# A re-dealt start-up of a fused sparse-attention and MLP kernel: load order, transposes, early scores and weight sums

## The chip, the core and the metric

The kernel runs on one core of a Trainium2 chip. TensorE (PE) multiplies, with its weight loads (PEld) beside it; VectorE (DVE), ScalarE (ACT) and GpSimd (POOL) do the elementwise work; POOL also issues the loads from memory, and SyncE (SP) the stores and the transposes by DMA. The metric is the device time of one execution in microseconds (us). Before the change the median of three runs was 321.06 us (319.18 to 321.56).

## The reference

Attention over 8 batches, 8 heads, 576 positions and head size 64, and then a two-layer MLP on the 4608 tokens that it gives. Heads 0 to 3 see a window of 32 positions ("local"); heads 4 to 7 see the earlier positions that are equal modulo 32 ("strided").

```python
mask_local = (rel >= 0) & (rel < stride)                      # stride = 32
mask_strided = (rel >= 0) & (pos[None, :] % stride == pos[:, None] % stride)
scores = np.where(masks, scale * q @ k.T, -1e9)
x = softmax(scores) @ v                                       # to 4608 x 512
h = x @ w_in                                                  # 512 x 2048
g = h * np.tanh(np.log1p(np.exp(h)))                          # Mish
out = g @ w_out                                               # 2048 x 512
```

## The kernel before

**Tiling.** The MLP works on 9 blocks of 512 tokens. Each block has a first product (x by `w_in`, into `gT` through Mish on ACT) and a second one (`gT` by `w_out`). From block 2 on the first product, and in all blocks the second, is done with seven half-size products instead of eight, which need sums of weights (`w_in_sums`, L343, into `wis` and into `w_in` itself; `w_out_sums`, L424, into `wos` and into `w_out` itself) and of activations (`x_sum`, L359; `g_sum`, L444, into `gs`); all these sums are two-input DVE instructions (L119). Blocks 0 and 1 use the ordinary first product, `plain` (L595): 16 column groups fc of 128, each four matmuls over the row groups cc; row groups 2 and 3 are the strided heads, 0 and 1 the local ones.

The second product of a block is 14 steps, called M1 to M14 below (`Mlp2.half`, L456): eight matmuls each, two steps for each of the seven products. In block 0 their order is n = 1, 2, 5, 6, 7, 3, 4. M1 and M2 need the first half of `w_out`, M3 (n = 2) the second half and a copy be<-al of what M2 left; M5 needs the changed `w_out` (sum w1), M7 the sums g1 and w2, M9 the sums w0 and g2, M11 the sum w3, M13 the sum g3.

**Attention**, one batch ahead of the MLP, in small steps put between the matmuls. For a batch, kind s (strided) or l (local): transposes of k and q; scores (`qk`) in three parts S0, S1, S2 and L0, L1, L2, each followed by two exps on ACT (L265) and a multiplication with the mask (`mask`, L271, on POOL or DVE); products with v (`pv`, L294) in five strided steps s0 to s4 and four local ones l0 to l3, each followed on DVE by a reciprocal (L298) and a multiplication (L303); and transposes of the result (`xt`) into `xT`: X0, X1 strided, Y0, Y1 local. `spread_v` and `share_v` (DVE copies) lay v out; s0 and its like need the first.

Batches 0 and 1 are transposed on PE (`t_step`, L189: 8 transposes for s, 12 for l, and a copy out of PSUM); for them raw k and q of batch 1 are kept in the tiles `hh` (strided), `xs` and a tile of the output pool (local), which have their own use only later. From batch 2 on `transpose_by_dma` (L174) does it from SP's queue.

**Order.** Everything runs in the order in which it is written, engine by engine (`manual_schedule`, L512). Loads go through POOL's queue in the order of L528 to L539, then L571, L576 and L614. The second product of block 0 is a written plan (L656): M is the next step, S0:CP is part S0 into PSUM pair C with the mask on POOL (D: DVE), k0:BD a transposing step into bank B copied by DVE, s0:B a pv step, X0:BA an xt step copied by ACT, v the laying out of v for batch 1 and the load of the next v, T the transposes by DMA, E the table load for exp on ACT, g2 and g3 sums of activations. Block 1 follows the plan SECOND (L737; p is a column group of `plain`, y its Mish, q0 to q5 the six score parts of batch 2 in the order S0 to S2, L0 to L2, all masked on POOL, v the next of the 13 pv and xt steps, k0 to k7 the sums of `w_in`, f the table load for Mish, n the sum g0), and from block 2 on MAIN (L732), where m is an M step of the block before, x0 to x3 the sums of x, and a to d and U, W, H the first product. Steps of v that a plan doesn't reach follow at its end.

PSUM has eight banks: SETS[0] and SETS[1] (be, al, ee each) and at0, at1 (A0, A1). B0 and B1 are the two be banks; pair A is A0 and A1, pair C the al and ee of SETS[0].

Of the kernel before, what the change touches and what calls it, by code (L numbers as in the profile page):

```python
# [12 lines left out]
AF = mybir.ActivationFunctionType  # L13
# [4 lines left out]
WQ = 96  # L18
CL, PL = 6, 96
SU = 80  # L20
# [25 lines left out]
def kernel(ctx, tc, q, k, v, moe_w_in, moe_w_out, out):  # L46
    nc = tc.nc
    B, H, S, D = q.shape
# [6 lines left out]
    PE, Po, Dv, Sc = nc.tensor, nc.gpsimd, nc.vector, nc.scalar  # L55
# [56 lines left out]
    def cast(eng, out_, in_):  # L112
        if eng is Sc:
            Sc.copy(out_, in_)  # L114
        else:
            eng.tensor_copy(out_, in_)
# [48 lines left out]
    def load_w_out(c0, c1):  # L165
        Po.dma_start(w_out[:, c0:c1, :], moe_w_out.rearrange("(fc p) o -> p fc o", p=128)[:, c0:c1, :])
# [7 lines left out]
    def transpose_by_dma():  # L174
        for src, dst in ((ks, kTs), (qs, qTs)):
            nc.sync.dma_start_transpose(
                dst[:, 0:16 * SU].rearrange("c (u n) -> c u n", u=16),
                src[0:SU].rearrange("p h x -> p (h x)"),
            )
        for src, dst, n in ((kl, kTl, 128), (ql, qTl, WQ)):  # L180
            nc.sync.dma_start_transpose(
                dst[:].rearrange("c (u n) -> c u n", u=12),
                src[0:n].rearrange("p h i d -> p (h i d)"),
            )
# [251 lines left out]
    class Mlp2:  # L436
# [19 lines left out]
        def half(self, n, u):  # L456
            z = (self.t + 1) % 2
            be, al, E = [x[:] for x in SETS[z]]
            W = lambda kk, j: w_out[:, 8 * kk:8 * kk + 8, 256 * j:256 * j + 256]
            G = self.G  # L460
            L, R, bank, start = {
                1: (G(0, 0), W(0, 0), al, True), 2: (G(0, 1), W(1, 0), be, False),
                3: (G(1, 1), wos[:, 2], E, False), 4: (gs[:, 1], W(1, 1), al, False),
                5: (gs[:, 0], W(0, 1), E, True), 6: (gs[:, 1], wos[:, 0], al, False),
                7: (gs[:, 2], wos[:, 1], al, False),
            }[n]
            for c in range(8):
                mm(
                    bank[:, 256 * u:256 * u + 256], L[:, c, 128 * u:128 * u + 128], R[:, c, :],
                    start=(start and u == 0 and c == 0), stop=(c == 7),  # L470
                )
            if u == 0:
                return
            r = 512 * self.t
            halves = lambda x: x.rearrange("p (u d) -> p u d", u=2)
            if n == 1:
                Sc.copy(be, al)
            elif n == 5:
                Sc.copy(o5[:], E)
            elif n == 6:  # L480
                Sc.copy(o2[:], al)
            elif n == 3:
                osb = self.out_tile(1)
                add(Dv, osb[:, :, 0:256], halves(E), halves(o2[:]))
            elif n == 7:
                osb = self.out_tile(1)
                add(Dv, osb[:, :, 256:512], halves(al), halves(o5[:]))
            elif n == 4:
                osb = self.out_tile(0)
                Sc.copy(osb[:, :, 0:256], halves(be))  # L490
                Sc.copy(osb[:, :, 256:512], halves(al))
                self.store(0)
# [19 lines left out]
    with tc.manual_schedule():  # L512
# [17 lines left out]
        load_vl(0)  # L530
        for c in range(4):
            load_w_in(512 * c, 512 * c + 512)
        load_w_out(0, 8)
        load_str(1, "ks", k)
        load_str(1, "qs", q)
        load_w_out(8, 16)
        load_loc(1, "kl", k, 128)
        load_loc(1, "ql", q, WQ)
        load_vl(1)  # L539

        Dv.memset(kTs[:, 0:16 * SU].rearrange("p (u n) -> p u n", u=16)[:, :, PN:], 0.0)
# [30 lines left out]
        a.bias("l", 0, PAIRS[1])  # L572
        a.bias("l", 1, PAIRS[2])
        t_step(0, "l", "q", 0, B0, Sc)
        t_step(0, "l", "q", 1, B1, Sc)
        load_qk(2)  # L576
        a.qk("l", 0, PAIRS[1], True)
        a.pv("s", *PV_S[0], A0)
# [27 lines left out]
        S2 = (2, 3)  # L606
        L2 = (0, 1)
# [18 lines left out]
        C = SETS[0]  # L626

        def go(plan):
            bank = {"A": A0, "a": A1, "B": B0, "C": C[1], "c": C[2]}
            eng = {"A": Sc, "D": Dv, "P": Po}  # L630
            for w in plan.split():
                f, x = w.split(":") if ":" in w else (w, "")
                if f == "M":
                    ms.pop(0)()
                elif f[0] in "kq" and f[1] in "01":
                    t_step(1, "l", f[0], int(f[1]), bank[x[0]], eng[x[1]])
                elif f[0] in "SL":
                    a.qk(f[0].lower(), int(f[1]), PAIRS[0] if x[0] == "A" else PAIRS[1])
                    a.mask(f[0].lower(), int(f[1]), eng[x[1]])
                elif f[0] in "sl":  # L640
                    n = int(f[1])
                    a.pv(f[0], *(PV_S if f[0] == "s" else PV_L)[n], bank[x])
                elif f[0] in "XY":
                    a.xt("s" if f[0] == "X" else "l", int(f[1]), bank[x[0]], eng[x[1]])
                elif f[0] == "g":
                    m2.g_sum(int(f[1]), Dv)
                elif f == "E":
                    Sc.preload_act_table(AF.Exp)
                elif f == "v":
                    spread_v(Dv)  # L650
                    share_v(1, Dv)
                    load_vs(2)
                elif f == "T":
                    transpose_by_dma()
# [90 lines left out]
        )  # L745

        for t in range(1, NBLK):
            run(SECOND if t == 1 else MAIN if t + 1 < B else PLAIN, t)
        last = Mlp2(NBLK - 1)
        st = last.steps((1, 5, 6, 2, 7, 3, 4))  # L750
        last.g_sum(1, Dv)
# [35 lines left out]
```

## Time and profile before

| What | us |
|---|---|
| median of three runs | 321.06 (319.18 to 321.56) |
| the profiled execution, its own time | 319.21 |
| its span, first to last instruction | 317.4 |
| PE, DVE, ACT, POOL busy | 288.6, 205.7, 201.2, 116.9 |
| local half of block 0's first product begins | 25.57 |
| second product of block 0 begins (M1) | 40.45 |
| local half of block 1's first product begins | 65.86 |
| M1 in block 2 begins | 90.56 |
| M1 in block 3 begins | 126.56 |
| M1 in block 4 begins | 156.37 |

Times in the profile count from the start of the span. The last five rows are where the timeline has the first matmul of that piece; the pieces between them are the stages that the change touches. In a line of the timeline the two numbers in front are start and duration, x is how many instructions were merged, and the bracket is how long the engine had been idle and what ended that.

### The profile page before, as it was taken

What the parts mean: (1) busy time and instruction counts of PE and PEld (TensorE: products, weight loads), DVE (VectorE), ACT (ScalarE), POOL (GpSimd) and SP (SyncE); (2) the same over time, 40 slices, a digit from 0 to 9 for tenths busy, and PEclk for the clock granted to TensorE, in tenths of its full rate; (3) what the DMA queues carried; (4) which work ended last, traced back from release to release, by engine and by line L of the source; (5) the groups of instructions that cost most, each with busy time, mean ns of one, the idle gap of its engine ahead of it and who ended that gap; (6) DMA issues with size and microseconds to landing.
All of it is one profiled execution on the core that took longest, in us unless ns stands there. A gap on an engine that the chain in (4) does not pass through costs nothing.

```text
span 317.4 us, 7701 instructions
## 1 busy us (share of the span) xinstructions
PE 288.6 (91%) x3218; PEld 228.4 (72%) x3224; DVE 205.7 (65%) x378; ACT 201.2 (63%) x357; POOL 116.9 (37%) x94
## 2 busy tenths in 40 slices
PE   8879679986994999999999999999999999999983
PEld 3554356833473798888888888988898887787773
DVE  2370396833888578768867794779578657747641
ACT  2587364357461768987887888788868526625630
POOL 8422355349504680298049607800930000000000
PEclk9999998999899899999999999999999999999999
DMA  7999999998990899589939993990030030002003
GB/s 105 182 206 206 204 183 138 95 243 130 150 115 0 114 231 169 32 142 214 169 41 176 205 137 64 213 107 0 2 134 2 0 119 15 3 34 101 0 2 133
DMA packets 97555, 35.85 MB, mean 113 GB/s; under 512 B 80800, under 2 KB 92896, under 8 KB 97520
## 3 DMA queue, kind: packets, MB, share of 16 engines
q0 software_dynamic: 60192, 17.67, 61.7%
q1 hardware_dynamic: 37184, 17.57, 27.7%
q8 instruction: 25, 0.41, 0.5%
q10 hardware_dynamic: 144, 0.12, 0.1%
q14 instruction: 10, 0.08, 0.1%
HBM read 35.51 MB, written 9.44 MB: 142 GB/s over the span
## 4 chain that ended last, share of the span: by engine, by line
PE 58%; DVE 16%; ACT 10%; DMA 10%; issue 4%; POOL 1%; DVEq 0%; ACTq 0%; POOLq 0%
PE al L125 29%; PE ee L125 14%; PE be L125 8%; DMA hh<-in_k_dram 7%; DVE hh L119 4%; DMA ql<-in_q_dram 3%; DVE gs L119 3%; ACT s L114 2%; ACT gT L414 2%; PE at L294 2%; PE at L125 2%; ACT gT L420 2%; DVE x_l L303 2%; DVE wis L119 1%; ACT be L401 1%
## 5 line engine op out<-in xcount | busy, mean ns | idle before, releaser
L125 PEld LDWEIGHTS <-w_in 128*128 128x128 bf16 x576 | 53.9, 98 | 23.6 <-issue 9.2
L271 POOL TENSOR_TENSOR Ps<-Ps,consts_sb 72x864 bf16<-72x864 bf16 (+1 forms) x20 | 36.8, 1859 | 87.1 <-ACT Ps L265 87.1
L125 PEld LDWEIGHTS <-gs 128*128 128x128 bf16 x576 | 55.8, 99 | 13.3 <-DVE gs L119 5.8
L125 PEld LDWEIGHTS <-gT 128*128 128x128 bf16 x432 | 41.0, 98 | 6.7 <-issue 0.4
L125 PE MATMUL al<-wos,gs 128*128 128x256 bf16 x288 | 36.4, 278 | 5.4 <-DVE gs L119 5.3
L125 PEld LDWEIGHTS <-wis 128*128 128x128 bf16 x348 | 33.1, 99 | 7.9 <-issue 3.3
L119 DVE TENSOR_TENSOR gs<-gT,gs 128x2048 bf16<-128x2048 bf16 x18 | 25.2, 1398 | 20.0 <-PE al L125 15.1
L271 POOL TENSOR_TENSOR Pl<-Pl,consts_sb 128x960 bf16<-128x960 bf16 (+1 forms) x20 | 33.5, 1701 | 0.8 <-ACT Pl L265 0.7
L125 PE MATMUL al<-xs,wis 128*128 128x256 bf16 x224 | 32.4, 272 | 0.8 <-ACT be L401 0.6
L125 PE MATMUL be<-xT,w_in 128*128 128x256 bf16 (+1 forms) x157 | 30.1, 311 | 2.8 <-ACT gT L693 1.3
L414 ACT ACTIVATE gT<-hh 128x1024 bf16<-128x1024 f32 x28 | 29.8, 1065 | 0.0
L125 PE MATMUL al<-xT,w_in 128*128 128x256 bf16 (+1 forms) x150 | 27.1, 299 | 1.9 <-ACT gT L420 1.7
L298 DVE RECIPROCAL rden<-at 72x7 f32<-72x7 f32 (+2 forms) x60 | 11.2, 187 | 21.6 <-PE at L294 18.1
L401 ACT COPY be<-al 128x512 f32<-128x512 f32 x28 | 16.4, 587 | 12.5 <-PE al L125 12.5
L420 ACT ACTIVATE gT<-al 128x512 bf16<-128x512 f32 x28 | 16.8, 599 | 11.0 <-PE al L125 11.0
L119 DVE TENSOR_TENSOR gs<-gT 128x2048 bf16<-128x2048 bf16 x18 | 21.9, 1217 | 0.0
L119 DVE TENSOR_TENSOR hh<-al,s 128x512 f32<-128x512 f32 x28 | 19.2, 684 | 2.9 <-PE al L125 2.5
L119 DVE TENSOR_TENSOR hh<-ee,s 128x512 f32<-128x512 f32 x28 | 19.2, 684 | 2.8 <-ACT s L114 1.9
L303 DVE TENSOR_TENSOR x_s<-at,rden 72x448 bf16<-72x448 f32 (+1 forms) x35 | 20.1, 574 | 1.2
L125 PE MATMUL ee<-wos,gT 128*128 128x256 bf16 x144 | 18.7, 277 | 0.0
L418 ACT ACTIVATE gT<-be 128x512 bf16<-128x512 f32 x28 | 15.9, 596 | 3.9 <-PE be L125 3.9
L125 PE MATMUL al<-xs,w_in 128*128 128x256 bf16 x112 | 16.8, 272 | 1.6 <-DVE hh L119 1.6
(137 smaller groups left out, 537.7 us busy)
## 6 DMA issues: line engine op xcount, KB each, us to landing
out_dram<-osb SPq DMA_DIRECT2D x18, 512.0 KB, 3.4
vraw<-in_v_dram POOLq DMA_DIRECT2D x8, 288.0 KB, 7.4
vl<-in_v_dram POOLq DMA_DIRECT2D x8, 288.0 KB, 9.6
w_in<-in_moe_w_in_dram POOLq DMA_DIRECT2D x4, 512.0 KB, 15.4
w_out<-in_moe_w_out_dram POOLq DMA_DIRECT2D x2, 1024.0 KB, 21.7
ql<-in_q_dram POOLq DMA_DIRECT2D x7, 288.0 KB, 12.9
kl<-in_k_dram POOLq DMA_DIRECT2D x5, 384.0 KB, 12.6
ks<-in_k_dram POOLq DMA_DIRECT2D x6, 288.0 KB, 10.0
```

Source lines behind the costliest of these rows:

```text
L114: Sc.copy(out_, in_)
L119: eng.tensor_tensor(out=out_, in0=a, in1=b, op=op)
L125: PE.matmul(o, lhsT=lhsT, rhs=rhs, start=start, stop=stop, skip_group_check=True)
L271: meng.tensor_tensor(out=pm, in0=pm, in1=mk[0:n, :].unsqueeze(1).unsqueeze(1).to_broadcast([n, 2, nu, w]), op=ALU.mult,)
L294: PE.matmul(po[:, n - n0, :], lhsT=pt[0:r, c0:c0 + 128], rhs=rhs, start=True, stop=True)
L298: Dv.reciprocal(rden[0:m, 0:nu], po[0:m, :, D])
L303: Dv.tensor_tensor(out=x[0:m, n0:n1, :], in0=po[0:m, :, 0:D], in1=rden[0:m, 0:nu].unsqueeze(2).to_broadcast([m, nu, D]), op=ALU.mult,)
L401: Sc.copy(be, al)
L414: Sc.activation(o[:, :, 256:512], h[:].rearrange("p i (u n) -> p (i u) n", u=2), AF.Mish)
L418: Sc.activation(o[:, 0:2, 0:256], two(be), AF.Mish)
L420: Sc.activation(o[:, 2:4, 0:256], two(al), AF.Mish)
```

## The change

It has these parts.

1. Loads: batch 1's strided k and q go ahead of the first half of `w_out`, its local k and q ahead of the second.
2. Batch 0: the copy of one local q transposition goes from ACT to DVE, where it stands behind `share_v`; the table load for Mish moves from before X0 to after the first three matmuls of block 0's first product.
3. First product of block 0: eight PSUM banks instead of six are dealt out; the strided half begins with three matmuls of row group 2 alone. Y1's copy goes to DVE. Batch 1's strided transposes follow column groups 8 to 11 (before: 9 to 12), and its local ones, which were steps k0, k1, q0, q1 of the second product's plan, follow groups 12 to 15, all copied by DVE. The sums g0 and w0 stand between the two.
4. Second product of block 0: a new plan. w1, g1, w2, w3 are spread between the steps; the copy be<-al of this block goes to DVE; the transposes by DMA come in two parts (Ts behind S2, Tl behind L2); batch 2's strided scores N0, N1, N2, masked on POOL, are added (before, q0 to q2 of block 1); the exp table is loaded at the start.
5. Block 1: q0 to q2 are gone; k1 comes early, k3 stays at the end, and k5 and k7 go to block 2, behind g3. Of the 13 v steps 12 stand in the plan; the last, Y1, follows it.

```diff
             if n == 1:
-                Sc.copy(be, al)
+                cast(Dv if self.t == 0 else Sc, be, al)
...
-        load_w_out(0, 8)
         load_str(1, "ks", k)
         load_str(1, "qs", q)
-        load_w_out(8, 16)
+        load_w_out(0, 8)
         load_loc(1, "kl", k, 128)
         load_loc(1, "ql", q, WQ)
+        load_w_out(8, 16)
         load_vl(1)
...
-        t_step(0, "l", "q", 1, B1, Sc)
+        t_step(0, "l", "q", 1, B1, Dv)
...
-        Sc.preload_act_table(AF.Mish)
...
-        for fc in range(4):
-            plain(0, fc, six[fc], S2)
-        a.xt("l", 0, A1, Sc)
-        plain(0, 4, six[4], S2)
-        plain(0, 5, six[5], S2)
-        a.xt("l", 1, A0, Sc)
+        deal = [B0, B1, A1] + SETS[1][1:] + SETS[0][1:] + [A0] + [
+            B0, B1, *SETS[1][1:], *SETS[0][1:], B0, B1
+        ]
+        for fc in range(3):
+            plain(0, fc, deal[fc], (2,))
+        Sc.preload_act_table(AF.Mish)
+        for fc in range(3):
+            plain(0, fc, deal[fc], (3,))
+        plain(0, 3, deal[3], (2, 3))
+        a.xt("l", 0, A0, Sc)
+        plain(0, 4, deal[4], (2, 3))
+        a.xt("l", 1, SETS[0][2], Dv)
+        plain(0, 5, deal[5], (2, 3))
...
         for fc in range(16):
-            plain(0, fc, six[fc % 6], (2, 3, 0, 1) if fc > 5 else L2)
-            if 9 <= fc <= 12:
-                t_step(1, "s", "kkqq"[fc - 9], fc % 2, (A0, A1)[fc % 2], Dv)
-        for n in range(4):
-            w_out_sums(n, Dv)
-            if n < 2:
-                m2.g_sum(n, Dv)
+            plain(0, fc, deal[fc], (2, 3, 0, 1) if fc > 5 else (0, 1))
+            if fc >= 8:
+                kind, n = "sl"[fc // 12], fc % 4
+                t_step(1, kind, "kq"[n // 2], n % 2, (A0, A1)[n % 2], Dv)
+            if fc == 11:
+                m2.g_sum(0, Dv)
+                w_out_sums(0, Dv)
...
         go(
-            "M M E S0:AP k0:BD S1:CP M k1:BD M S2:AD q0:BD M q1:BD M v L0:CP M g2 L1:AP s0:B M L2:CD "
-            "s1:B M M g3 s2:B M s3:A s4:a T M l0:c X0:BA M l1:C l2:A X1:aA M l3:B Y0:cA Y1:CA"
+            "E M M S0:CP w1 g1 M S1:AP M w2 M S2:CD Ts w3 v M L0:AP g2 M L1:CP s0:B M s1:B L2:AD Tl M s2:B g3 s3:A s4:a M "
+            "l0:B M X0:A l1:a M N0:CP X1:B l2:A M l3:a N1:CP Y0:B M Y1:A N2:CP"
         )
...
         SECOND = (
-            "p0 q0 p1 q1 p2 s q2 p3 q3 p4 q4 p5 v q5 f D V R y0 v v p6 v y1 p7 k0 k2 v y2 v p8 y3 k4 k6 v p9 y4 v p10 y5 v "
-            "p11 y6 v p12 y7 v p13 y8 v p14 y9 v p15 y10 y11 y12 y13 y14 y15 n k1 k3 k5 k7"
+            "p0 s p1 q3 p2 q4 p3 q5 p4 p5 f D V R v v y0 v p6 y1 v p7 v y2 p8 k0 k2 v y3 p9 k4 k6 k1 v y4 v p10 y5 v "
+            "p11 y6 v p12 y7 v p13 y8 p14 y9 v p15 y10 y11 y12 y13 y14 y15 n k3"
         )
...
+            if t == 2:
+                plan = plan.replace("g3", "g3 k5 k7")
```

More of the change, by code (lines that the diff above doesn't have):

```diff
@@ L172, in share_v, with transpose_by_dma @@
         cast(eng, vl[b % 2][0:32, :, 1:NW, 0:D], vl[b % 2][96:128, :, 0:NW - 1, 0:D])
[L174 to L184, printed above, removed]
+    def transpose_by_dma(kinds="sl"):
+        if "s" in kinds:
+            for src, dst in ((ks, kTs), (qs, qTs)):
+                nc.sync.dma_start_transpose(
+                    dst[:, 0:16 * SU].rearrange("c (u n) -> c u n", u=16),
+                    src[0:SU].rearrange("p h x -> p (h x)"),
+                )
+        if "l" in kinds:
+            for src, dst, n in ((kl, kTl, 128), (ql, qTl, WQ)):
+                nc.sync.dma_start_transpose(
+                    dst[:].rearrange("c (u n) -> c u n", u=12),
+                    src[0:n].rearrange("p h i d -> p (h i d)"),
+                )
     kTl0 = kTl[:, 0:2 * (32 + S)].rearrange("c (t n) -> c t n", t=2)
@@ L605 @@
         six = [B0, B1] + SETS[1][1:] + SETS[0][1:]
-        S2 = (2, 3)
-        L2 = (0, 1)
-        for fc in range(4):
-            plain(0, fc, six[fc], S2)
-        a.xt("l", 0, A1, Sc)
-        plain(0, 4, six[4], S2)
-        plain(0, 5, six[5], S2)
-        a.xt("l", 1, A0, Sc)
+        deal = [B0, B1, A1] + SETS[1][1:] + SETS[0][1:] + [A0] + [
[11 more added lines that the diff above has]
+        plain(0, 5, deal[5], (2, 3))
         load_vl(2)
@@ L617 @@
         for fc in range(16):
-            plain(0, fc, six[fc % 6], (2, 3, 0, 1) if fc > 5 else L2)
-            if 9 <= fc <= 12:
-                t_step(1, "s", "kkqq"[fc - 9], fc % 2, (A0, A1)[fc % 2], Dv)
-        for n in range(4):
-            w_out_sums(n, Dv)
-            if n < 2:
-                m2.g_sum(n, Dv)
+            plain(0, fc, deal[fc], (2, 3, 0, 1) if fc > 5 else (0, 1))
[5 more added lines that the diff above has]
+                w_out_sums(0, Dv)
         ms = m2.steps((1, 2, 5, 6, 7, 3, 4))
         C = SETS[0]
+        nx = Attn(2)
         def go(plan):
@@ L634, in go @@
                     ms.pop(0)()
[L635 to L639, printed above, removed]
+                elif f[0] in "SLN":
+                    at, kind = (nx, "s") if f[0] == "N" else (a, f[0].lower())
+                    at.qk(kind, int(f[1]), PAIRS[0] if x[0] == "A" else PAIRS[1])
+                    at.mask(kind, int(f[1]), eng[x[1]])
                 elif f[0] in "sl":
@@ L643, in go @@
                 elif f[0] in "XY":
-                    a.xt("s" if f[0] == "X" else "l", int(f[1]), bank[x[0]], eng[x[1]])
+                    a.xt("s" if f[0] == "X" else "l", int(f[1]), bank[x], Sc)
                 elif f[0] == "g":
                     m2.g_sum(int(f[1]), Dv)
+                elif f[0] == "w":
+                    w_out_sums(int(f[1]), Dv)
                 elif f == "E":
@@ L652, in go @@
                     load_vs(2)
-                elif f == "T":
-                    transpose_by_dma()
-        go(
-            "M M E S0:AP k0:BD S1:CP M k1:BD M S2:AD q0:BD M q1:BD M v L0:CP M g2 L1:AP s0:B M L2:CD "
-            "s1:B M M g3 s2:B M s3:A s4:a T M l0:c X0:BA M l1:C l2:A X1:aA M l3:B Y0:cA Y1:CA"
+                elif f[0] == "T":
+                    transpose_by_dma(f[1])
+        go(
+            "E M M S0:CP w1 g1 M S1:AP M w2 M S2:CD Ts w3 v M L0:AP g2 M L1:CP s0:B M s1:B L2:AD Tl M s2:B g3 s3:A s4:a M "
+            "l0:B M X0:A l1:a M N0:CP X1:B l2:A M l3:a N1:CP Y0:B M Y1:A N2:CP"
         )
@@ L747 @@
         for t in range(1, NBLK):
-            run(SECOND if t == 1 else MAIN if t + 1 < B else PLAIN, t)
+            plan = SECOND if t == 1 else MAIN if t + 1 < B else PLAIN
+            if t == 2:
+                plan = plan.replace("g3", "g3 k5 k7")
+            run(plan, t)
         last = Mlp2(NBLK - 1)
```

## The prediction

> **What bounds the kernel now.** The first page gives PE 91% busy, and the chain that ended last is 58% PE. So I asked where PE is idle, stage by stage (stretch, length, then busy time of PE, PEld, DVE, ACT, POOL, granted clock, DMA):
>
> ```profile
> 0.00:25.50 25.50, 20.83 (x255) 11.55 (x257) 10.20 (x38) 13.77 (x28) 14.21 (x21) 1.00 1.17 167
> 25.50:40.30 14.80, 12.24 (x83) 6.00 (x84) 3.62 (x6) 8.33 (x16) 4.44 (x5) 1.00 1.26 204
> 40.30:65.20 24.90, 21.67 (x303) 16.81 (x303) 19.64 (x36) 11.54 (x24) 10.41 (x7) 0.93 2.15 139
> 65.20:90.20 25.00, 20.87 (x199) 10.85 (x202) 12.26 (x28) 15.41 (x29) 15.57 (x12) 0.93 1.51 171
> 90.56:126.56 36.00, 31.19 (x365) 26.20 (x364) 27.82 (x47) 22.09 (x40) 15.95 (x12) 0.95 1.13 124
> 126.56:156.37 29.81, 29.45 (x366) 25.60 (x364) 22.48 (x43) 24.54 (x44) 16.57 (x12) 1.00 1.07 139
> ```
>
> Block 3 (last row) is PE-bound: 29.45 of 29.81 us. Block 2 does the same work in 36.0, and each earlier stage leaves PE 2.6 to 4.8 us idle. All edits lie in these stages, and what they save isn't given back, since later blocks wait on PE. The timeline names the waits that end last there:
>
> ```profile
> 12.83 0.76 POOL L133 DMA_DIRECT2D hh<-in_k_dram  x1 [1.21 <-DMA ql<-in_q_dram]
> 14.13 1.01 POOL L133 DMA_DIRECT2D hh<-in_q_dram  x1 [0.55 <-DMA vraw<-in_v_dram]
> 16.50 0.48 DVE L116 COPY vl<-vl 32x1280 bf16<-32x1280 bf16 x1 [1.60 <-DMA vl<-in_v_dram]
> 34.20 0.43 PE L196 MATMUL at<-consts_sb,hh 72*128 72x72 bf16 x8 [2.44 <-DMA hh<-in_k_dram]
> ...
> 75.47 1.28 ACT L709 ACT_TABLE_LOAD   x1
> 77.41 1.50 PE L125 MATMUL be<-xT,w_in 128*128 128x512 bf16 x4 [1.33 <-ACT gT L693]
> ...
> 96.03 3.86 POOL L271 TENSOR_TENSOR Ps<-Ps,consts_sb 72x864 bf16<-72x864 bf16 x2 [10.04 <-ACT Ps L265]
> 96.26 1.95 DVE L119 TENSOR_TENSOR xs<-xT 128x512 bf16<-128x512 bf16 x1
> 98.13 2.83 DVE L119 TENSOR_TENSOR gs<-gT,gs 128x2048 bf16<-128x2048 bf16 x1
> 101.02 2.97 PE L125 MATMUL al<-wos,gs 128*128 128x256 bf16 x16 [4.45 <-DVE gs L119]
> ```
>
> The four stalls: batch 1's raw k (34.20), exps and table load before Mish (77.41), the late g1 in block 2 (101.02), and, in block 0's second product, DVE. The DVE and POOL rows show something that I use throughout: the x sum takes 1.95 us where its like takes 0.42, and g1 2.83 instead of 1.22, just while two masks run; the masks take 3.86 instead of 2 x 1.79. In block 3 three masks take 5.80 (4.83 in block 1), with a g3 of 1.61 among them. So **a two-input DVE sum and a POOL mask exclude each other**, and whoever waits goes next: they alternate.
>
> **Prologue: +1.4 us.** The q copy now stands on DVE behind `share_v`, which waits for its load until 16.50. It runs 16.96 to 17.71 (a local copy on DVE is 0.75), where ACT had finished at 15.92. The second local score waited for it until 15.97 and now waits until 17.75. DVE's run of reciprocals and products, contiguous from 16.91, then starts at 18.45: 1.54 late. X0's copy no longer waits for the Mish table (ACT had it 18.76 to 20.04), but the table is now behind ACT's six l2 pieces (1.32 us): these run 23.65 to 24.97, the table to 26.25, Y0's copy (0.64) to 26.89. The local half begins at 26.95 instead of 25.57. Its cover before was the wait for k at 34.20; that goes too.
>
> **First product: -0.7.** POOL keeps eight loads open, as its issues show, each released by the landing eight earlier: the four parts of `w_in` landed at about 19.0, 21.5, 24.1 and 27.0, and the first half of `w_out` at 32.3, as they released later issues. So 0.52 MB takes 2.5 us. Batch 1's strided k and q then land 2 to 2.9 us after 27.0, at 29 to 30, and local k and q at 35.7 and 37.2, when the same bytes have passed. Three full column groups (0.865 each) and six halves end group 8 at 32.1: no wait, -2.44. Four local transposing steps are added at 0.37 (24 such transposes took 0.70), +1.5; and the third waits 0.25 for its bank, as DVE does g0 and w0 (1.22 each) ahead of the copies. M1 begins at 41.1 (before 40.45).
>
> **Second product: +2.5.** Counted from M1. DVE copies the last q (to 0.85), waits for M2, copies be<-al (2.0 to 2.7), does w1 to 3.85. S0's exps end at 3.15, so its mask waits for w1 and runs 3.85 to 5.65; by alternation g1 5.65 to 6.85, mask S1 to 8.65, w2 to 9.85. M7, which PE reaches at 7.2, waits 2.7 us for w2. Then on DVE mask S2 (0.45), w3, the spreading (0.68), `share_v` (0.48), g2 to 13.8; POOL's next load sits in its queue behind the spreading, so no mask intrudes there. s0 waits for the spreading until 12.15; s1 for its bank until s0's product, 14.65. Mask L2 waits for masks L0 and L1 on POOL until 17.6, and s2's product is behind it. From there DVE is contiguous (s2, g3, s3, s4, two output sums, l0 to l3) to 25.5, and ACT ends with N1's exps, Y0, two output copies and Y1 at 27.9. Block 1's local half begins there; before it took 25.41. Without mask waits DVE would save 3.4 us: ends -0.9 and +2.5, and I take the upper, as the alternation is what the rows show.
>
> **Block 1: -3.5.** Before, six score parts and their exps stood between p0 and the Mish table; p6 came 11.55 us after the start. Now three remain: p0, p1, q3 (exps 1.03), q4, q5, the table 5.25 to 6.55 after the start, y0 0.6, and s2 between: p6 at 7.85, a gain of 3.7. From p6 on there were 13.1 us, of them about 1.2 at a low clock (p6 took 1.50 instead of 1.03). Now ten groups (8.65), s3 to l3 with transposes (2.15), and 1.7 us in which l1 waits for X1's copy, behind k4, k6 and k1 (0.69 each): 13.3 with small waits. 24.7 becomes 21.2.
>
> **Block 2: -4.0.** DVE now has n, k3, Y1's copy, x0, x1, the two v copies, x2, and g1 ends 5.5 us after M1, before the first mask (96.03 is 5.5 after M1 too, but g2 is already issued at 5.43) and before M7 at 6.1: the 4.45 stall and its slow restart (2.97 instead of 1.91) go. But k5 and k7 aren't free: after g3 (9.65) each waits for a mask (1.8, 1.3), so the output sum comes at 14.15 and s0's product at 15.7, where block 3 has 13.0. PE wants s2 at 13.9: a new stall of 1.9, with 0.3 for clock. 36.0 becomes 32.0. Bounds: 0.7 if no mask intervenes, 4.0 if mask S0 gets in ahead of g2.
>
> [...] In this trace PE idle 1.85 of the 4 us up to 48 was followed by a granted clock of 0.69 up to 52. [...]
>
> **Sum.** +1.4 - 0.7 + 2.5 - 3.5 - 4.0 = -4.3. Against the profiled execution (319.21, span 317.4) that is 314.9; the median shown is 1.85 above it, 316.8 by that. I forecast **316.0**, between them. A measurement here can tell about 1%, 3.2 us, from no change.
>
> **Rivals.** *A: the masks don't hold up block 0's second product* (the sums fall between them): 3.4 less, 312.6. For: before, masks of 1.8 us ran there at full speed. Against: they met copies from PSUM, not sums. *B: mask S0 gets in ahead of g2 in block 2*: stall 4.0 and 1.4 of clock instead of 2.2 in all, +3.2, 319.2. The margin is 0.15 us. *C: the change doesn't do what it says*: batch 1's k still lands at 34.2, for two loads issued 1.3 us apart (12.83 and 14.13) both landed 34.1 to 34.3, so transfers overlap; then group 8 waits 2.1: 318.1. Against: `w_in` landed in even steps. *D, slower: the second half of `w_out` lands late.* It is issued at 21.7 instead of 16.8, behind 0.59 MB more. By bytes it lands at 42.0, where local q landed before; by its old 22.1 us from issue, at 43.8. w1 and M3 want it at 43.7, and each us beyond costs one, as all DVE work queues behind w1. At 48 the gain is gone; landing with batch 2's loads, about 49 to 52, gives +1 to +4, say 322.
>
> **How the numbers follow.** Forecast 0.42, A 0.24, B 0.14, C 0.10, D 0.10. Faster by over 1% (below 316.9 on the scale of 316.0): A and most of the forecast, 0.60. Within 1%: B, C, some of the forecast and D, 0.31. Slower: 0.09. Range 310.5 (A with the 0.7 bound of block 2) to 321.5 (B, C, and D's beginning).
>
> **What would show it.** Local half at 26.95 behind a table load at 25.0; group 8's transposes without a wait; M1 at 41.1; M7 waiting for w2; block 1's local half at 69.0; p6 7.85 later; block 2 at 90.2 with no wait for g1 but one for s0's product; block 3 at 122.2. The forecast is wrong if sums and masks don't alternate as in block 2, or a load lands 2 us from where its bytes put it.

## The result, and the profile after

The changed kernel took **325.51 us** (median of four runs, 324.65 to 326.13; the kernel before 320.96 beside it): a ratio of 1.0149, interval 1.0103 to 1.0196. It is 1.5% slower, where 316.0 was forecast. Ratios and their intervals are taken from the runs of a kernel that lie within 1.5% of its fastest; of the versions below only the first with its masks on DVE had others, two of ten, and without them its median is 315.42 us. The profiled execution took 326.13 us (span 324.3, granted clock 0.957). Lines of the changed kernel stand two further down than before (the masks at L273, the products with v at L296 and L305).

Stage by stage, in the columns that were used for before (stretch, length, busy time of PE, PEld, DVE, ACT, POOL, granted clock, DMA):

```profile
0.00:28.55 28.55, 23.47 (x256) 12.78 (x256) 11.51 (x40) 12.59 (x26) 14.84 (x22) 0.88 1.17 171
28.55:42.76 14.21, 14.21 (x132) 7.05 (x133) 6.10 (x9) 8.67 (x16) 5.22 (x5) 1.00 1.41 199
42.76:74.92 32.16, 23.42 (x290) 18.13 (x287) 28.08 (x34) 13.01 (x27) 13.44 (x7) 0.79 1.47 126
74.92:96.18 21.26, 18.41 (x170) 9.46 (x170) 12.26 (x28) 12.86 (x25) 12.24 (x11) 1.00 1.51 167
96.18:133.46 37.28, 31.36 (x368) 26.46 (x366) 31.58 (x47) 21.92 (x40) 17.90 (x12) 0.91 1.03 122
```

| Stage | before | after | forecast change | measured | miss |
|---|---|---|---|---|---|
| to the local half of block 0 | 25.57 | 28.55 | +1.4 | +2.98 | +1.6 |
| first product, block 0 | 14.88 | 14.21 | -0.7 | -0.67 | 0.0 |
| second product, block 0 | 25.41 | 32.16 | +2.5 | +6.75 | +4.25 |
| block 1 | 24.70 | 21.26 | -3.5 | -3.44 | +0.1 |
| block 2 | 36.00 | 37.28 | -4.0 | +1.28 | +5.3 |
| sum | | | -4.3 | +6.90 | +11.2 |

Block 3 takes 29.81 us in both. DVE is the row to look at: 28.08 of 32.16 us busy in the second product (19.64 of 24.90 in the row shown of before), 31.58 in block 2 (27.82 before), with no more instructions than before (34 for 36, and 47 for 47). The timeline names what it was "busy" with. First PE: the places that answer to the stalls shown of before (batch 1's k at 34.20, g1 at 101.02), and the two new ones.

```profile
33.74 0.42 PE L198 MATMUL at<-consts_sb,hh 72*128 72x72 bf16 x8
...
52.18 1.03 PE L125 MATMUL al<-wos,gs 128*128 128x256 bf16 x8 [1.91 <-DVE wos L119]
...
61.21 0.54 PE L296 MATMUL be<-vs,Ps 72*128 72x65 bf16 x7 [4.67 <-DVE x_s L305]
...
102.03 1.91 PE L125 MATMUL al<-wos,gs 128*128 128x256 bf16 x16
...
115.52 0.54 PE L296 MATMUL at<-vs,Ps 72*128 72x65 bf16 x7 [5.51 <-DVE x_s L305]
```

The wait for k is gone, and so is the one for g1. In their place PE waits 4.67 us in the second product and 5.51 us in block 2, each time for the multiplication behind a product with v. Then DVE and POOL, in the same timeline:

```profile
46.53 2.84 DVE L119 TENSOR_TENSOR gs<-gT,gs 128x2048 bf16<-128x2048 bf16 x1
49.29 2.83 DVE L119 TENSOR_TENSOR wos<-w_out 128x2048 bf16<-128x2048 bf16 x1
...
54.76 5.63 DVE L119 TENSOR_TENSOR gs<-gT 128x2048 bf16<-128x2048 bf16 x1
...
54.52 0.79 POOL L148 DMA_DIRECT2D vraw<-in_v_dram  x1 [3.48 <-DVE vs L116]
55.34 3.95 POOL L273 TENSOR_TENSOR Pl<-Pl,consts_sb 128x960 bf16<-128x960 bf16 x2
...
105.34 7.45 DVE L119 TENSOR_TENSOR wis<-w_in 128x1024 bf16<-128x1024 bf16 x1
112.82 1.28 DVE L119 TENSOR_TENSOR wis<-w_in,wis 128x1024 bf16<-128x1024 bf16 x1
```

g1 and w2 waited for one mask each, as forecast. But g2, 1.2 us of work, took 5.63 and ended 1.1 us after mask L1: both local masks had passed it, though it had been issued first. k5, 0.68 us of work, took 7.45. The masks beside it, one by one:

```profile
104.30 2.79 POOL L273 TENSOR_TENSOR Ps<-Ps,consts_sb 72x864 bf16<-72x864 bf16 x1
107.05 1.27 POOL L273 TENSOR_TENSOR Ps<-Ps,consts_sb 72x576 bf16<-72x576 bf16 x1
108.28 2.00 POOL L273 TENSOR_TENSOR Pl<-Pl,consts_sb 128x960 bf16<-128x960 bf16 x1
110.24 1.99 POOL L273 TENSOR_TENSOR Pl<-Pl,consts_sb 128x960 bf16<-128x960 bf16 x1
```

k5 began its wait at 105.34, during S1; then S2, L0 and L1 went by, and it came in only ahead of L2 and ended at 112.79. Behind it and k7 in DVE's queue stood the output sum, which began at 114.03, 17.85 us after M1 (14.15 was forecast), and s0's multiplication.

### The profile page after: what moved, and what is told of

Same layout as the page of the kernel before. It is cut to its first block, busy times and chain, and to the rows that moved or that the text cites. A ratio compares the mean times of both kernels' runs of the same rounds, so it can differ in the third digit from the quotient of the medians.

```text
span 324.3 us, 7711 instructions
## 1 busy us (share of the span) xinstructions
PE 292.3 (90%) x3224; PEld 230.7 (71%) x3224; DVE 221.3 (68%) x381; ACT 199.1 (61%) x354; POOL 119.9 (37%) x94
## 4 chain that ended last, share of the span: by engine, by line
PE 62%; DVE 17%; ACT 10%; issue 5%; DMA 4%; POOL 1%; DVEq 0%; ACTq 0%; POOLq 0%
PE al L125 30%; PE ee L125 15%; PE be L125 10%; DVE hh L119 4%; DMA vl<-in_v_dram 4%; DVE wis L119 3%; DVE gs L119 3%; PE at L296 2%; ACT s L114 2%; ACT gT L416 2%; PE at L125 2%; ACT gT L422 2%; DVE wos L119 1%; ACT be L403 1%; DVE x_l L305 1%
## 5 line engine op out<-in xcount | busy, mean ns | idle before, releaser
L273 POOL TENSOR_TENSOR Ps<-Ps,consts_sb 72x864 bf16<-72x864 bf16 (+1 forms) x20 | 40.0, 2021 | 96.6 <-ACT Ps L267 96.5
L125 PEld LDWEIGHTS <-gs 128*128 128x128 bf16 x576 | 57.0, 101 | 11.4 <-issue 2.1
L125 PE MATMUL al<-wos,gs 128*128 128x256 bf16 x288 | 38.1, 285 | 2.7 <-DVE wos L119 1.9
L119 DVE TENSOR_TENSOR gs<-gT,gs 128x2048 bf16<-128x2048 bf16 x18 | 25.4, 1409 | 19.4 <-PE al L125 14.5
L273 POOL TENSOR_TENSOR Pl<-Pl,consts_sb 128x960 bf16<-128x960 bf16 (+1 forms) x20 | 33.4, 1698 | 1.2 <-ACT Pl L267 1.1
L125 PE MATMUL be<-xT,w_in 128*128 128x256 bf16 (+1 forms) x160 | 30.2, 311 | 1.0 <-ACT xT L114 0.8
L119 DVE TENSOR_TENSOR gs<-gT 128x2048 bf16<-128x2048 bf16 x18 | 26.3, 1462 | 0.0
L296 PEld LDWEIGHTS <-Ps 72*128 72x128 bf16 x256 | 12.0, 102 | 14.2 <-issue 12.3
L305 DVE TENSOR_TENSOR x_s<-at,rden 72x448 bf16<-72x448 f32 (+1 forms) x35 | 20.1, 575 | 1.2
L125 PE MATMUL al<-w_out,gs 128*128 128x256 bf16 x144 | 18.8, 286 | 0.1
```

The costliest lines, as they stand in the source:

```text
L119: eng.tensor_tensor(out=out_, in0=a, in1=b, op=op)
L125: PE.matmul(o, lhsT=lhsT, rhs=rhs, start=start, stop=stop, skip_group_check=True)
L273: meng.tensor_tensor(out=pm, in0=pm, in1=mk[0:n, :].unsqueeze(1).unsqueeze(1).to_broadcast([n, 2, nu, w]), op=ALU.mult,)
L296: PE.matmul(po[:, n - n0, :], lhsT=pt[0:r, c0:c0 + 128], rhs=rhs, start=True, stop=True)
L305: Dv.tensor_tensor(out=x[0:m, n0:n1, :], in0=po[0:m, :, 0:D], in1=rden[0:m, 0:nu].unsqueeze(2).to_broadcast([m, nu, D]), op=ALU.mult,)
```

## Experiments

Theory H after this: a row of ready masks on POOL keeps a DVE sum out for longer than one mask, and costs all 9.5 us missed in the second product and block 2. Rivals: the sums were slow for a reason of their own (place in the code, operands, POOL's load ahead of them), or the prologue's loss is what counts.

### The two places

k5 and k7 put behind x3 of block 2, where no mask runs:

```diff
-                plan = plan.replace("g3", "g3 k5 k7")
+                plan = plan.replace("x3", "x3 k5 k7")
```

> The changed kernel with one edit: in block 2 the sums k5 and k7 follow x3 instead of g3, where POOL issues loads and runs no masks. Theory H (a row of masks that stand ready on POOL keeps a two-input DVE sum out until the row pauses): k5 takes 0.7 us instead of 7.45, s0's product comes in time, PE's stall of 5.5 us and the slow clock after it go; block 2 (M1 to M1) falls from 37.1 to 30 to 31, the kernel from 325.5 to about 319. Rival R (sums and masks alternate, as forecast; k5's 7.45 us had another cause, something that k5 itself waits for): k5 stays long in its new place, or the stall moves to the next sum; block 2 stays above 34.

g2 put ahead of the v copies, and so ahead of POOL's load and the local masks:

```diff
-   ... w3 v M L0:AP g2 M L1:CP ...
+   ... w3 g2 v M L0:AP M L1:CP ...
```

> The changed kernel with one edit: in block 0's second product g2 stands ahead of the spreading of v (and so ahead of the load and the masks L0 and L1 on POOL) instead of behind M6 and L0. Theory H: g2 takes 1.2 us instead of 5.63; s0 comes 1.1 later, s1 some 3.3 earlier; the second product falls from 32.2 to 28 to 29, the kernel by 3 to 4 us, to about 322. Rival R: g2's wait wasn't the masks; the second product stays within 1 us of 32.

Measured: with k5 and k7 late 318.3 us (317.54 to 319.55), ratio 0.9927 (0.9899 to 0.9954); with g2 early 321.89 (320.53 to 323.21), ratio 1.0040 (1.0019 to 1.0060). DVE in the timeline of the first:

```profile
103.06 1.44 DVE L119 TENSOR_TENSOR gs<-gT,gs 128x2048 bf16<-128x2048 bf16 x1 [1.31 <-PE al L125]
113.55 0.68 DVE L119 TENSOR_TENSOR wis<-w_in 128x1024 bf16<-128x1024 bf16 x1
114.27 0.69 DVE L119 TENSOR_TENSOR wis<-w_in,wis 128x1024 bf16<-128x1024 bf16 x1
```

and of the second:

```profile
53.17 1.21 DVE L119 TENSOR_TENSOR gs<-gT 128x2048 bf16<-128x2048 bf16 x1
```

The same sums take 0.68, 0.69 and 1.21 us where no mask runs, so they are not slow by themselves. Block 2 falls from 37.28 to 30.22 us (M1 at 95.26 and 125.48), the second product from 32.16 to 27.77 (27.9 was forecast). Two moves of one line each are worth 7.2 and 3.6 us, and the first alone makes the change a gain.

### How long a mask row keeps a sum out

> A kernel that leaves the whole computation out (it writes zeros): four scenes of POOL masks (128x960, two inputs) against DVE sums (128x1024, two inputs, 0.68 us alone). 1: six masks all ready, a sum asked for in the first. 2: six masks whose data ACT hands on one by one, each ready before the mask ahead of it ends; a sum in the first. 3: three sums in a row, masks come up during the first. 4: a load on POOL with four masks ready behind it, a sum asked for during the load. Theory H: in 1, 3 (from the first mask on) and 4 the sum ends only behind the last mask, 8 to 12 us; in 2 it may get in behind the first. Rival R: in all scenes the sum ends behind the first mask that it meets, 2 to 3 us, and the third sum of scene 3 behind the next.

Here no sum waited for more than one mask: asked for at 14.92 it took 1.50 us, at 30.22 1.62, and of three in a row (3.69 us together) the third came in behind the first mask. That speaks against H as it stood. The scene with the load says nothing, for its sum ran ahead of the load (58.77 against 58.94). These masks were plain, 128 partitions by 960. A second kernel of this kind used the kernel's own:

> A kernel that computes nothing of the reference: it writes zeros to the output, and lets sums on DVE and masks on POOL meet in nine scenes, on tiles of zeros, all masks of a scene ready at once. Scenes 1, 2, 5 and 6 have the kernel's masks in its order, S0 S1 S2 L0 L1 L2 (with the broadcast operand); scene 3 only the local ones, scene 4 plain 128x960 masks. A copy out of PSUM holds the DVE back until the first mask runs; then come g3 and k5 (1, 3, 4), k5 alone (2), two plain sums (5), g3 and g2 (6). Scene 7: a load on POOL, then L0 L1 L0 L1, and on DVE the v copy, then g2; scene 8 the same without the load. Theory A (alternation): no sum waits for more than one mask, so no sum takes over 2.7 us in any scene (0.7 to 1.2 of its own and a rest of a mask). Theory B (masks with the broadcast operand keep a sum out that is already waiting when a mask takes over): k5 takes over 5 us in scene 1, the second plain sum over 5 us in scene 5, g2 over 5 us in 6, but no sum over 2.7 us in scene 4. Theory C (a sum whose two operands are strided parts of one tile is kept out, whatever the mask): k5 takes over 5 us in scenes 1 to 4 and g2 in 6 and 8, the plain sums not over 2.7 in scene 5. Theory D (POOL's load ahead is what put g2 off): g2 takes over 4 us in scene 7 and under 3.2 us in 8.

Its first scene, POOL and then DVE:

```profile
30.44 1.81 POOL L83 TENSOR_TENSOR Ps<-Ps,consts_sb 72x864 bf16<-72x864 bf16 x1 [29.99 <-ACT consts_sb L118]
32.21 1.81 POOL L83 TENSOR_TENSOR Ps<-Ps,consts_sb 72x864 bf16<-72x864 bf16 x1
33.98 1.27 POOL L83 TENSOR_TENSOR Ps<-Ps,consts_sb 72x576 bf16<-72x576 bf16 x1
35.21 2.00 POOL L83 TENSOR_TENSOR Pl<-Pl,consts_sb 128x960 bf16<-128x960 bf16 x1
37.16 2.98 POOL L83 TENSOR_TENSOR Pl<-Pl,consts_sb 128x960 bf16<-128x960 bf16 x1
...
31.49 6.80 DVE L89 TENSOR_TENSOR gs<-gT,gs 128x2048 bf16<-128x2048 bf16 x1
38.21 2.48 DVE L89 TENSOR_TENSOR wis<-w_in 128x1024 bf16<-128x1024 bf16 x1
```

g3 asks during S0, and S1, S2 and L0 go by. Only when L0 ends does it come in (mask L1 shows the wait: 2.98 instead of 1.99). Scenes 2, 5 and 6, with k5, a plain sum and g3 again, did the same: 6.33, 6.27 and 6.86 us. So theory A falls, and C with it, as the plain sum is held as long. In scene 3 (local masks only) and 4 (plain ones on tiles of their own) every sum came in behind one mask, which fits B only in part, since scene 3 has the broadcast operand too. Scenes 7 and 8 say nothing on D: in 7 the load had ended 4 us before the masks began, and in 8 g2 began 1 us ahead of them. What is left is the 72 partitions of the S masks:

> A kernel that computes nothing of the reference: it writes zeros to the output, and lets one DVE sum meet a row of six POOL masks, on tiles of zeros, in eleven scenes. Scenes 1 to 4 have six equal masks of 72, 128, 96 and 64 partitions (864 elements each, broadcast operand), 5 six plain ones on 72 partitions; 6 alternates 72-partition masks with the local ones of 128; 7 is scene 1 with a sum on 72 partitions; 8 has the kernel's masks with their scores handed on by copies on ACT, one by one, and g3, k5; 9 and 10 have the two v copies on DVE, a load on POOL behind them, g2 on DVE and four ready masks behind the load, of 128 partitions (9) and of 72 (10). Theory E (a mask on fewer than 128 partitions hands the memory on to the next mask without letting a sum in): the sum takes over 9 us in scenes 1, 3, 4, 5 and 7 (all masks of the row), under 3 in scene 2, and in 6 it is let in after the first local mask; in 8 it waits for L0 as when all masks are ready (6.8 us). Theory F (only the order of starts decides, not the partitions): scenes 1 to 5 agree with each other within the difference of the masks' own times. For the kernel's 5.63 us of g2: over 4 us in scene 9 if the load ahead is the cause, under 3.2 if not.

```profile
30.45 1.81 POOL L83 TENSOR_TENSOR Q<-Q,consts_sb 72x864 bf16<-72x864 bf16 x1 [30.01 <-ACT consts_sb L136]
31.50 1.84 DVE L102 TENSOR_TENSOR gs<-gT,gs 128x2048 bf16<-128x2048 bf16 x1
32.34 2.68 POOL L83 TENSOR_TENSOR Q<-Q,consts_sb 72x864 bf16<-72x864 bf16 x1
35.10 1.81 POOL L83 TENSOR_TENSOR Q<-Q,consts_sb 72x864 bf16<-72x864 bf16 x1
36.99 1.81 POOL L83 TENSOR_TENSOR Q<-Q,consts_sb 72x864 bf16<-72x864 bf16 x1
...
102.54 3.80 DVE L102 TENSOR_TENSOR gs<-gT,gs 128x2048 bf16<-128x2048 bf16 x1
103.27 1.99 POOL L96 TENSOR_TENSOR Pl<-Pl,consts_sb 128x960 bf16<-128x960 bf16 x1
```

Scene 1 (72 partitions) let the sum in behind the first mask, and so did 2 to 5 and 7, at 128, 96, 64 and 72 partitions: theory E, as put, falls, and the agreement is what theory F asked for. But these masks work on one and the same tile, and the starts show what that does: 1.89 us apart for 1.81 us of work, a pause of 0.08 between masks. In the scenes that held a sum out, the next mask on its other tile starts 0.04 us before the last one's end. In scene 6, where 72-partition and local masks alternate on two tiles, the sum is passed over behind the 72-partition mask (3.80 us) and let in behind the local one. In scene 8, with masks handed on one by one by ACT, k5 came in behind S0 (2.31 us).

What is shown: **where POOL paused only 0.08 us between two masks, a waiting sum came in every time; where masks followed without a pause, it was let in at some of them and passed over by up to three in a row.** Behind a 72-partition mask without a pause it always was, when all were ready; behind L0 it came in in these kernels, but g2 and k5 were passed over there in the changed one. In the changed kernel, too, g3 came in between S0 and S1 in every block. What decides these cases stays open, and so does the part of POOL's load: in scenes 9 and 10 g2, issued 0.23 us behind the start of a load with ready masks behind it, ran at once (1.23 us).

### The prologue

The copy of q back on ACT, the Mish table back ahead of X0's copy:

```diff
-        t_step(0, "l", "q", 1, B1, Dv)
+        t_step(0, "l", "q", 1, B1, Sc)
...
+        Sc.preload_act_table(AF.Mish)
         a.xt("s", 0, A1, Sc)
...
         for fc in range(3):
             plain(0, fc, deal[fc], (2,))
-        Sc.preload_act_table(AF.Mish)
```

> The changed kernel with the prologue of before: the second local q copy on ACT, the table load for Mish ahead of X0. Theory: the copy behind share_v cost 1.75 us of PE idle and with it the clock (0.88 over the stage), so the local half of block 0 begins at 25.6 to 26.1 instead of 28.55 and the kernel gains 2.5 to 3, to about 322.7. Rival: the loads of batch 1 bind instead (strided k lands at 29 to 30, group 8 would want it at 29.7 to 30.7; local k at 36 to 37, wanted at 34.5), and M1 begins only 1 to 1.5 earlier than 42.76.

> The changed kernel with k5 and k7 behind x3 of block 2 and the prologue of the kernel before (q copy of batch 0 on ACT, Mish table ahead of X0's copy); g2 in its old place. With k5 and k7 alone moved the ratio to the kernel before was 0.9927, with the prologue alone 1.0144 against 1.0149 for the changed kernel. If the prologue is worth its 2.1 us and block 2's held sums gave it back: M1 of block 0 at 39.5 to 40.7 with a granted clock of 1.00 from 16 to 24 us where loads come in time, ratio 0.985 to 0.988. If the prologue's gain is lost in block 0's second product whatever block 2 does: M1 of block 2 stays at 94.5 to 96, ratio 0.991 to 0.994.

Alone: 325.34 us, ratio 1.0144 (1.0112 to 1.0176); M1 comes 2.1 us earlier (40.62), but block 2 with k5 among the masks takes 38.6 instead of 37.3, and the time is that of the changed kernel. With k5 and k7 late: 317.27 us (316.78 to 317.73), ratio 0.9885 (0.9843 to 0.9928), against 0.9927 without. M1 of block 0 is at 41.65 (42.17 without) and of block 2 at 94.5 (95.26). The intervals overlap, so that a gain of some 0.5 to 1.3 us is likely and not shown. What the prologue lost is shown by the windows and the timeline of the changed kernel:

```profile
12.00:16.00 4.00, 3.37 (x64) 2.23 (x63) 2.02 (x3) 2.46 (x6) 1.82 (x2) 1.00 1.81 186
16.00:20.00 4.00, 2.14 (x56) 1.70 (x56) 2.45 (x6) 1.78 (x4) 1.38 (x2) 1.00 1.23 203
20.00:24.00 4.00, 3.27 (x46) 2.61 (x45) 3.80 (x13) 2.06 (x6) 1.00 (x2) 0.51 1.24 206
24.00:28.00 4.00, 4.00 (x23) 1.74 (x22) 0.55 (x1) 3.08 (x8) 1.64 (x2) 0.64 1.25 203
...
17.86 0.20 PE L125 MATMUL al<-qTl,kTl 64*128 64x96 bf16 x1 [2.02 <-DVE qTl L116]
...
25.18 1.28 ACT L612 ACT_TABLE_LOAD   x1
26.89 0.42 PE L318 MATMUL at<-consts_sb,x_l 96*128 96x96 bf16 x6
28.04 0.46 DVE L116 COPY xT<-ee 128x576 bf16<-128x576 bf16 x1 [3.48 <-PE ee L318]
```

and of a kernel with the old prologue (the composite below that is the first to have it):

```profile
16.00:20.00 4.00, 3.26 (x76) 2.50 (x76) 3.27 (x9) 3.57 (x8) 1.38 (x2) 1.00 1.23 204
20.00:24.00 4.00, 3.21 (x42) 2.07 (x42) 2.69 (x10) 3.21 (x10) 0.90 (x1) 1.00 1.24 206
```

PE waits 2.02 us for the q copy at 17.86, is busy 2.14 of 4 us, and the next 4 us run at a clock of 0.51. All six kernels with the new prologue show 0.50 to 0.54 there; of the seven with the old one four show 1.00 and three 0.50 to 0.58. In one of those four (k5 and k7 late) the matmuls were slow all the same: 14 products with v took 0.95 us at 17.93, where the changed kernel has 0.60. And in one of the six, g2 early, the wait for the q copy was only 0.6 us, and the clock fell to 0.50. So the fall comes without the wait too; whether the wait makes it likelier is not shown.

### The sums of w_in alone

The kernel before, with nothing of the change but k1 moved into block 1, k3 behind n, k5 and k7 behind x3 of block 2:

> The kernel before, with nothing of the change but the sums of w_in spread: k1 in block 1, k3 behind n, k5 and k7 behind x3 of block 2 (not behind g3). If the 4.45 us wait for g1 in block 2 with its slow restart is all that separates block 2 (36.0 us) from block 3 (29.8): block 2 takes 30.2 us, as with the changed kernel's k5 and k7 behind x3, and the time is 315 to 315.8, 1.7% faster. If the masks hold x2 and g1 back again (1.95 and 2.83 us in the kernel before), a stall of 1 to 2 us is left and the time is 317 to 318.

315.66 us (314.36 to 316.55), ratio 0.9834 (0.9802 to 0.9866). Block 2 takes 30.2 us, as expected. This alone gains more than the changed kernel with its worst place mended: of everything in the change, this was the part with the gain, if put past the masks. That the rest of the change adds anything to it is not shown, for no version below has an interval that lies under this one's.

### Versions that take the sums out of the masks' way

First all of it: k5 and k7 late, g2 early, the copy be<-al on ACT, and w1 and w2 moved up.

```diff
-   E M M S0:CP w1 g1 M S1:AP M w2 M S2:CD Ts w3 v M L0:AP g2 M L1:CP
+   E w1 M M S0:CP g1 w2 M S1:AP M M S2:CD Ts w3 g2 v M L0:AP M L1:CP
```

> Changed kernel with k5 and k7 behind x3 of block 2, g2 ahead of the v copies in block 0's second product, the copy be<-al of block 0 on ACT as before, and w1 and w2 moved up on DVE (w1 ahead of M1, w2 behind g1). If the three places each cost what they seemed to: M7's wait for w2 (1.9 us) goes, block 0's second product takes 26 us (32.2 in the changed kernel, 27.8 with g2 alone moved), block 2 30.2, and the time is 312.5 to 313.5, 2.4% under the kernel before. If mask S0 on POOL only takes the place of the wait (g1 and w2 meet S0 and S1 anyway): M7 still waits over 1 us, the second product 27.5 to 28, time 314.5 to 315.

314.62 us (313.33 to 316.12), ratio **0.9806** (0.9762 to 0.9851): the lowest median, though the intervals of seven others overlap its own. M7's wait is gone, but s0's product waits 2.31 us for the v copies that now stand behind w3 and g2. The second product took 28.76 us, where 26 was hoped for and g2's move alone gave 27.77: moving w1, w2 and the copy as well gained nothing there. The same with the old prologue:

> The kernel of the run before this one with the prologue of the kernel before as well: the q copy of batch 0 on ACT, the Mish table ahead of X0's copy. If the 2.1 us that this gained up to block 0's second product are kept where nothing downstream gives them back, it is 2 us faster than that kernel: 310.5 to 311.5, 3% under the kernel before. If the prologue's gain is always given back (by loads that land when they did), it is within 0.5 us of it.

314.91 us, ratio 0.9817 (0.9793 to 0.9841): no gain, though M1 came 3.5 us earlier (39.4). S0's product then waited 3.51 us for the v copies. So these were put right behind w1 and g1 (`E w1 g1 v M M S0:CP w2 ...`):

> As the run with the prologue of the kernel before and all DVE sums early, and in addition the two v copies of batch 1 right behind w1 and g1, ahead of M1 of block 0's second product. There s0's product waited 3.51 us for them. If that wait sets the end of the second product: 3 us faster than that kernel, 311.5 to 312. If the strided transposes of batch 2 by DMA, which the next scores waited 2.16 us for, come no earlier, the wait moves there and the time stays within 0.7 us of 314.9.

316.79 us (314.9 to 317.11), ratio 0.9889 (0.9832 to 0.9946). The wait moved, and grew; w2 was now the sum in the masks' way:

```profile
47.00 0.75 POOL L148 DMA_DIRECT2D vraw<-in_v_dram  x1 [7.98 <-DVE vs L116]
47.85 1.83 POOL L273 TENSOR_TENSOR Ps<-Ps,consts_sb 72x864 bf16<-72x864 bf16 x1
49.62 1.82 POOL L273 TENSOR_TENSOR Ps<-Ps,consts_sb 72x864 bf16<-72x864 bf16 x1
51.40 1.99 POOL L273 TENSOR_TENSOR Pl<-Pl,consts_sb 128x960 bf16<-128x960 bf16 x1
...
47.25 7.23 DVE L119 TENSOR_TENSOR wos<-w_out 128x2048 bf16<-128x2048 bf16 x1
```

The load, which waits for the v copies, held the masks back until S0 and S1 were both ready; L0 was ready (49.34) before S1 began, and all three went by w2; M7 waited 6.43 us. Like g2 in the changed kernel, w2 was issued a quarter of a us after the load's start. So the load was put behind mask L1, in the kernel with only k5 and k7 late:

> The changed kernel with k5 and k7 behind x3 of block 2, and in block 0's second product POOL's load of v behind mask L1 instead of ahead of mask L0; g2 stays in its place behind the v copies. In the changed kernel and with k5 and k7 alone moved g2 took 5.63 us. If the load is what keeps g2 out: g2 takes 1.2 to 3.2 us (at most one mask), block 0's second product 28 to 29.5 us, the time 315 to 316. If the row of ready masks does it: mask L0 starts ahead of g2, which waits for the ends of L0 and L1 and takes 3.5 to 5 us; the second product 30.5 to 32, the time 317 to 318.5.

317.57 us, ratio 0.9899 (0.9842 to 0.9955), M1 of block 2 at 95.28 where it was 95.26. Here g2 ran beside a load with no masks behind it, and took 1.23 us; but masks L0 and L1 now met the DVE mask S2 (2.25 us instead of 0.44) and the v copy (2.48 instead of 0.68), and s0's product waited 4.36 us. Here the load alone held no sum, and moving it moved the loss. Last, none of batch 1's masks on POOL in that stage (batch 2's N0 to N2 stay there, behind the last sum):

```diff
-   E M M S0:CP w1 g1 M S1:AP M w2 M S2:CD Ts w3 v M L0:AP g2 M L1:CP
+   E w1 g1 w2 M M S0:CD M S1:AD M M S2:CD Ts v w3 g2 M L0:AD M L1:CD
```

> The run with all DVE sums early (314.6 us), with the masks of block 0's second product all on DVE, in its own order (w1, g1, w2, masks S0, S1, S2, the v copies, w3, g2, masks L0, L1), so that no sum there can meet a mask on POOL. DVE gains four masks of 0.5 to 0.75 us, 2.6 us of work. If sums held out by POOL's masks are what is left of the loss there, no sum of this stage takes over 1.25 us, s0's wait for the v copies falls from 2.31 us to under 1.2, the second product is 1.5 to 3 us shorter and the time 311.5 to 313.5. If DVE's own queue sets the end, the four masks cost what they save: 314 to 316.

> All together: k5 and k7 behind x3, the masks of block 0's second product on DVE with the sums early, the copy be<-al on ACT, the prologue of the kernel before. The kernel with all of this but the prologue had a ratio of 0.985 and M1 of block 2 at 91.65. If the prologue's 2 us are kept: M1 of block 0 at 39.5 to 40.7, of block 2 at 89 to 90, ratio 0.975 to 0.979, 312 to 313 us. If the transposes of batch 2 by DMA, which N0's scores waited 1.93 us for, don't come earlier, the gain ends there: M1 of block 2 at 91 or later, ratio 0.981 to 0.985.

The first, with the new prologue: 316.16 us (313.78 to 320.0), ratio 0.9848 (0.9807 to 0.9890); no sum of the stage took over 1.23 us, a mask on DVE 0.35 to 0.65, and M1 of block 2 came at 91.65, 49.0 us after that of block 0. With g2 alone moved it was as soon (42.38 and 91.42), so the masks on DVE gave nothing more; s0's product now kept PE waiting 2.88 us. With the old prologue too: 316.09 us (313.55 to 318.13), ratio 0.9854 (0.9806 to 0.9902), with M1 of block 0 at 42.33, not at the 39.5 to 40.7 hoped for, and of block 2 at 95.27. The profiled execution was the slowest of the six, 318.13 us. PE and SP there:

```profile
51.30 5.86 SPq L177 DMA_TRANSPOSE qTs<-qs  x1
...
66.92 0.22 PE L125 MATMUL al<-qTs,kTs 64*128 64x72 bf16 x1 [5.50 <-DMA qTs<-qs]
```

N0's scores, which the change moved into this stage, need batch 2's q transposed by DMA. PE waited for it 1.19, 2.16, 1.93 and 5.50 us in four of these versions, and 1.36 in the kernel before with the sums spread; in these five it landed 13.0 to 15.8 us after its issue at about 51 (10.3 to 14.5 in the other eight profiles). Where DVE's sums are out of the way this is the next bound of the start-up, and the likely reason, though not a tested one, why five versions end within 1% of each other.

## Why the prediction was wrong

**What bounds the kernel now** was read rightly: the four stalls were the ones to gain from, and three of them went. The sum failed on what took their place.

**Prologue, +1.4: mis-sized by the clock.** The chain was as described up to the table: q copy at 17.07 to 17.81 on DVE, the first reciprocal at 18.63, the table from 25.18 to 26.46 (26.25 forecast). But then PE, not ACT, was last: the granted clock fell to 0.51 and 0.64, PE was busy all of the 4 us from 24 to 28, and Y0's transposes came only at 26.89, with the table done, and Y1's copy at 28.04. So the local half began at 28.55 and not at 26.95; only 0.2 us of that were the table's. The prediction priced a restart in block 2 (0.3), and left it out here, though the same row of before (clock 0.69 after 1.85 us idle) said it. In the changed kernel no wait of PE from 14 to 24 us was above 2.02 us (the one at 17.86), and the clock from 20 to 24 was 0.51. What makes it fall stays open.

**First product, -0.7: right** (-0.67). Group 8's transposes began at 33.74 without a wait, those of local k at 38.34. Batch 1's strided k and q landed at 28.9 and 29.1 (29 to 30 forecast), local k and q at 35.1 and 36.6 (35.7 and 37.2): the loads landed where their bytes put them, and rival C was not it.

**Second product, +2.5: the step "by alternation" failed for g2.** M7 did wait for w2 (1.91, forecast 2.7), and M1 to the local half was 27.77 us with g2 moved, against 27.9 forecast: the rest of the sum held. "No mask intrudes there" was the wrong sentence: the load that was to keep the masks off lasted until 55.31, 0.55 us after g2's issue, and g2 lost to both masks behind it. Rival D, `w_out` late, was not it: w1 began at 45.40 without waiting for its load.

**Block 1, -3.5: right** (-3.44): p6 came at 82.91, 7.99 us after the start (7.85 forecast), without its wait.

**Block 2, -4.0: the same step failed.** g2 was issued ahead of mask S0 (101.44 against 101.64) and the stall for g1 went, so rival B was not it. "Each waits for a mask (1.8, 1.3)" was wrong: k5 waited for the rest of S1 and for three masks more, 6.8 us. The stall that was put at 1.9 us became 5.51, and M13 and M14 behind it took 3.32 us instead of 1.9 at the fallen clock (0.53 from 112 to 116 us, 0.62 to 120), for which 0.3 was allowed: together 4.7 of the 5.3 missed. The prediction had named this as a sign of being wrong, that sums and masks don't alternate.

**Where the rule came from.** In the profile of before every sum that met two masks came in between S0 and S1, in all blocks; from this "whoever waits goes next" was concluded. It was the wrong generalisation: no sum of before was asked for while S1, S2 or L0 ran on POOL with the next one ready. Nor did the order of issue decide who was next: k5, issued at 105.34, ran behind S2, L0 and L1, which started at 107.05, 108.28 and 110.24.

The range ended 4 us under the result, for the bounds of block 2 were set by alternation too ("0.7 if no mask intervenes, 4.0 if mask S0 gets in ahead of g2"). A whole row of masks, some 8 us from S1 to L2 by their single times, had to be among the bounds. No rival had it: the slower case named a load. Two figures beside the sum don't come out of its own rows, and neither bore on the miss: B's margin is put at 0.15 us, where g2 at 5.43 and the mask at 5.47 after M1 (96.03) give 0.04, and 0.20 was measured, and A with the 0.7 bound gives 311.1, not 310.5.

## What to carry to other kernels

Price a DVE sum that can meet POOL masks at the whole row of masks that are ready or about to be, not at one (k5 took 7.45 us among them and 0.68 away from them, g2 5.63 and 1.21): put it where no mask runs. Masks on DVE were shorter (0.60 to 0.65 us, 1.8 to 2.0 on POOL), but they gave no more than moving the sums did. A habit seen between two instructions of one kind is not a rule; look in the trace for a case with three in a row before building a sum on it. And leave room for the clock: in the changed kernel its fall to 0.51 cost the prologue some 1.4 us by the estimate above (the 1.6 missed less the table's 0.2), as much as the whole loss forecast for it.

## What the runs showed of the hardware

- A DVE copy between SBUF tiles was held by a POOL mask as sums are, 2.48 us instead of 0.68 for the v copy, and so was a mask on DVE, 2.25 instead of 0.44.
- On POOL a mask on another tile started 0.04 us before the last one's end, one on the same tile 0.08 us after it. The second let a waiting DVE sum in each time (six scenes).
- A POOL load of 0.79 us by itself didn't hold a DVE sum (1.23 us beside it).
